# Linear attention and routed experts on one core: more buffers for the loads of q, k and v

## The chip, the cores and the metric

The kernel runs on one core of one Trainium2 chip. The metric is the device time of one execution in microseconds (us), lower is better; a time below is the median of several executions unless it is said to be the profiled one.

## The reference, cut to what matters

Eight batches with eight heads each, 576 positions, head width 64. Queries and keys are projected to 128 features, shifted by the row's largest magnitude and exponentiated with both signs; the attention is linear, so the keys and values are first summed up into one small matrix per head. The result, 4608 rows of 512, goes through a layer of eight experts of which each row takes one, or none.

```python
def phi(x):
    proj = np.einsum('bhsd,df->bhsf', x, w_phi)
    proj = proj - np.max(np.abs(proj), axis=-1, keepdims=True)
    return np.concatenate([np.exp(proj), np.exp(-proj)], axis=-1)
q_p, k_p = (phi(q), phi(k))
kv = np.einsum('bhsf,bhsd->bhfd', k_p, v)
z = np.sum(k_p, axis=2)
num = np.einsum('bhsf,bhfd->bhsd', q_p, kv)
den = np.einsum('bhsf,bhf->bhs', q_p, z)[..., None] + 1e-06
...
x = attn_out.transpose(0, 2, 1, 3).reshape(B * S, H * D)
do_compute = x @ w_skip > 0            # the other rows are returned as they are
e_idx = argmax(x @ w_gate)             # one expert for each row
y = gate_w * (relu(x @ w1[e]) @ w2[e])
out[do_compute] = x + y
```

## The kernel before, in words

**Two stages.** The attention takes the first 373 us of the profiled execution, the experts the rest. The change touches only the attention's loads.

**Units and steps.** The attention works on units: four heads of one batch, once as a k unit (k rows with their v) and once as a q unit. There are 16 units of each kind, k0 to k15 and q0 to q15. Each is cut into five items: item 0 is the tail of 64 positions of each head, items 1 to 4 are the others. The program walks in steps (line 732); in one step one item of the k stream and one of the q stream are worked on, the q stream six steps behind. One unit of each kind takes five steps, about 22 us here.

**The path of an item.** SyncE (SP) issues the load of a unit's raw rows as four transfers of 144 KB together, `raw` (`st_load`, L261 to L269). VectorE (DVE) transposes it into `xT`, or for the tail into `xTt` (L296, L298). TensorE (PE) projects it into `ps_P` (L321). DVE takes the row's largest magnitude `m` (L328) and subtracts it, which gives `u` (L331). ScalarE (ACT) exponentiates: k items straight from `u` into `ek` or `ekt` (L346, L347), q items after PE has transposed `u` into the one bank `ps_U` (L367, then L373 and L374 into `eq`). For k, PE multiplies `ek` with the values `v` into `ps_K` (L389, and L396 with the tail `vt`), and GpSimd (POOL) sums `ek` (L354). For q, PE multiplies `eq` with the unit's sums `kva` (L487, tails L466), and DVE divides: `den`, `rec`, `xm`, `lgm` (L438 to L450).

**After every batch** (two units) comes `post` (L515): DVE finds the expert of each row, PE counts ranks (L582), DVE turns them into indices (`RKH`, L607), POOL makes `OP` and `rhs` of them (L605, L617) and PE multiplies these (L628). Batches with an odd number have the tails of both batches in it and are longer. SP stores the batch's rows: half of `xm` after the first unit (L505), the rest with L566 to L568, and the output rows with L637 and L642 (1 MB and twice 128 KB).

**Buffers.** A tile has a number of buffers and takes them in turn; a load into a buffer waits until the last reader of the tile that had it before is done. `raw` has four for k and q units together, taken in the order k0, k1, q0, k2, q1, k3, q2 and so on. `v` has the two of its pool `ld`, `vt` is one of two tiles that are cleared once at the start (L94, L105) and written in two halves (L282).

**The order of the instructions** on PE is written out by hand for nearly the whole attention (L735). On DVE, POOL, SP and ACT a scheduler sets it when the program is built: it runs the program on a model of the engines and puts next what would be ready then. A transpose of a tail can so stand far ahead of the step that asks for it. On the chip each engine works through its list in that order, and an instruction whose data isn't there holds all that stand behind it.

Of the kernel before, what the change touches and what calls it, by code (L numbers as in the profile page):

```python
# [8 lines left out]
F32 = mybir.dt.float32  # L9
# [9 lines left out]
P = 128  # L19
# [5 lines left out]
def kernel(  # L25
# [13 lines left out]
    B, H, S, D = q.shape  # L39
# [34 lines left out]
    ac = pools["ac"]  # L74
# [16 lines left out]
    nc.scalar.activation(out=warm, in_=warm, func=AF.Exp)  # L91


    vts = [ac.tile([P, 2, 2, D], F32, name="vt%d" % j) for j in range(2)]  # L94
    wsrc = ac.tile([P, NF], F32, name="wsrc")

    NP2 = H // 2
# [132 lines left out]
    with actx:  # L230
        ld, hl, zp, up, ep, kvp, xp = (pools[nm] for nm in ("ld", "hl", "zp", "up", "ep", "kvp", "xp"))
# [16 lines left out]
        for b in range(B):  # L248
            for kind in ("k", "q"):
                for hq in range(NQ):  # L250
                    u = Unit()
# [8 lines left out]

        def st_load(u):  # L261
            src = kv_in[u.kind]
            u.raw = ld.tile([P, 2, 18, 32], F32, tag="raw", name="raw", bufs=4)
            for hd in range(2):
                for dh in range(2):
                    r = hd * 64 + dh * 32
                    nc.sync.dma_start(
                        out=u.raw[r:r + 32].rearrange("p r t c -> p (r t) c"),
                        in_=src[u.g, hd][:, :, dh * 32:dh * 32 + 32])  # L269

        def st_loadv(u):
            u.v = ld.tile([P, 4, 4 * D], F32, tag="v", name="v")
            u.vt = vts[u.g % 2]
            for h in range(4):
                nc.sync.dma_start(
                    out=u.v[:, h, :].rearrange("p (g c) -> p g c", c=D),
                    in_=vu[u.g, 0:4 * P, h, :].rearrange("(g p) c -> p g c", p=P))
# [423 lines left out]
        for dh in range(2):  # L701
            nc.scalar.dma_start(
                out=wsrc[dh * 64:dh * 64 + 64],
                in_=w_phi)
        st_load(streams[0][1][0])
        load_gate()

# [12 lines left out]
        def f_t():  # L720
            for items, us, off in streams:
                s = now[0] - off
                if s == CFG["ql"]:
                    st_load(us[0])
                if 0 <= s < n:
                    u, i = items[s]
                    st_t(u, i)
                    if i == 0 and s // 5 + 1 < len(us):
                        st_load(us[s // 5 + 1])

        man = None
        for t in range(n + OFF + LA):
            if CFG["man"] and t == CFG["man"][0]:
                man = ExitStack()
                man.enter_context(tc.manual_schedule(engines={mybir.EngineType.PE}))  # L735
            if CFG["man"] and t == CFG["man"][1]:
                man.close()
            now[0] = t
            for w, f in [x for x in later if x[0] <= t]:
                later.remove((w, f))  # L740
                f()
            for c in CFG["order"]:
                if c == "Z":
                    run_stage(LZ, st_z)
                elif c == "A":
                    run_stage(LA, st_aug)
                elif c == "U":
                    run_stage(LU, f_use)
                elif c == "E":
                    run_stage(LE, f_exp)  # L750
                elif c == "P":
                    st_proj()
                else:
                    f_t()
            run_stage(LU - 3, lambda u, i: st_loadv(u) if (i == 0 and u.kind == "k") else None)
            run_stage(CFG["vtl"], lambda u, i: st_loadvt(u) if (i == 0 and u.kind == "k") else None)
            if t == CFG["at"]:
                setup_aug()
            if t == 1:
                setup()  # L760
# [431 lines left out]
    with tc.manual_schedule():  # L1192
# [4 lines left out]
        for k, (w, x, c) in enumerate(steps):  # L1197
# [5 lines left out]
            while nxt < len(steps) and nxt <= k + 5 and (nxt <= k + 1 or parted[nxt] <= T[k] + 1.0):  # L1203
                w_, x_, c_ = steps[nxt]
                v = nxt not in CFG["gp"] if x_[0] == "E" else not (
                    (x_[0] == "C" and w_ == 1 or x_[0] == "S") and c_ % 2 == 1)
# [87 lines left out]
```

## Time and profile before

| what | value |
|---|---|
| median of 3 runs | 664.88 us (663.05 to 673.61) |
| the profiled execution | 655.62 us |
| its span, first to last instruction | 653.8 us |
| PE busy, of the span | 578.6 us (88%) |
| DVE busy, of the span | 515.1 us (79%) |
| loads of raw k and q | 64 transfers of 144 KB each, median 3.1 and 4.1 us from issue to landing |
| loads of v | 64 transfers of 128 KB, median 2.7 us |

A row of the timeline gives the start and the length of a piece of work in us, its engine and line, what is written from what, and in brackets how long the engine stood idle ahead of it and what ended that. "SPq" rows are transfers that SP issues; their length is the time that issuing took, not that of the transfer. A row of the waits gives the sum of such idle times, how many there were, and the longest.

### The profile page before, as it was taken

Reading aid. Unit: us, or ns where it says so; the run is one execution under the profiler, and the core shown is the slowest. Engines: PE = TensorE matmul, PEld = TensorE weight load, DVE = VectorE, ACT = ScalarE, POOL = GpSimd, SP = SyncE. Lnnn points to the kernel's source line nnn. Section 1 sums busy time; section 2 is a strip of 40 time slices with the busy share of each in tenths; the row PEclk is TensorE's granted clock in tenths of the full one; section 3 lists DMA queues with packets and bytes.
Section 4 is the critical chain, followed back from the end, with each engine's and each line's share of the span. In section 5 each row is a group of like instructions: output and inputs, shape, how many; then the busy total and the mean of one; then the engine's idle time right before and its main releaser. Section 6 shows DMA issues by size and latency. Waiting matters only on the chain. (4 is left out here: it accounts for less than half of the span.)

```text
span 653.8 us, 18749 instructions
## 1 busy us (share of the span) xinstructions
PE 578.6 (88%) x7486; PEld 473.8 (72%) x7486; DVE 515.1 (79%) x1084; ACT 329.4 (50%) x649; POOL 360.3 (55%) x389
## 2 busy tenths in 40 slices
PE   4769988979988899889899899879999898999994
PEld 2557767756776677667677788769988777998893
DVE  5668987998888969879898669995787888866761
ACT  3345554555455455445554634414457735774630
POOL 5545454654565554635666254995565958268221
PEclk9899999989999999999899989789999999999998
DMA  9977566746765756555316288858767797776300
GB/s 155 167 122 142 112 143 124 164 105 125 182 122 99 189 108 146 116 115 142 106 34 223 80 242 306 291 192 258 213 184 224 235 313 245 246 246 231 132 18 28
DMA packets 245369, 108.33 MB, mean 166 GB/s; under 512 B 192161, under 2 KB 226081, under 8 KB 245280
## 3 DMA queue, kind: packets, MB, share of 16 engines
q1 hardware_dynamic: 240768, 97.58, 57.5%
q0 software_dynamic: 3200, 9.45, 4.2%
q8 instruction: 60, 0.98, 0.6%
q10 hardware_dynamic: 1312, 0.08, 0.1%
q14 instruction: 29, 0.24, 0.1%
HBM read 83.86 MB, written 24.02 MB: 165 GB/s over the span
## 5 line engine op out<-in xcount | busy, mean ns | idle before, releaser
L354 POOL TENSOR_TENSOR z<-ek 128x512 f32<-128x512 f32 x64 | 81.4, 1272 | 122.9 <-ACT ek L347 85.2
L203 POOL TENSOR_TENSOR w<-wraw_c,w 128x256 fp32r<-128x256 f32 x124 | 112.6, 942 | 52.0 <-ACT w L198 52.0
L198 ACT ACTIVATE w<-wraw_c 128x1024 fp32r<-128x1024 f32 x96 | 97.5, 1050 | 4.2 <-DMA wraw_c<-in_moe_w_dram 3.2
L203 DVE TENSOR_TENSOR w<-wraw_c,w 128x1024 fp32r<-128x1024 f32 x65 | 86.6, 1342 | 13.1 <-ACT w L198 12.1
L331 DVE TENSOR_TENSOR u<-ps_P,m 128x1024 f32<-128x1024 f32 (+2 forms) x86 | 89.6, 1042 | 4.9 <-DVE m L328 0.5
L328 DVE TENSOR_REDUCE m<-ps_P 128x8 f32<-128x1024 f32 (+2 forms) x86 | 88.4, 1028 | 6.0 <-PE ps_P L321 5.8
L321 PE MATMUL ps_P<-wsrc,xT 64*64 64x128 f32 x2048 | 81.9, 292 | 12.0 <-DVE xT L298 7.0
L487 PEld LDWEIGHTS ps_O<-kva,eq 128*64 128x64 f32 x2048 | 74.5, 136 | 16.7 <-issue 5.5
L487 PE MATMUL ps_O<-kva,eq 128*64 128x74 f32 x2048 | 77.6, 228 | 3.9 <-DVE lgm L450 3.8
L321 PEld LDWEIGHTS ps_P<-wsrc,xT 64*64 64x64 f32 x2048 | 59.8, 140 | 28.0 <-issue 18.5
L389 PE MATMUL ps_K<-ek,v 128*64 128x256 f32 x512 | 73.9, 408 | 0.0
L851 POOL DMA_INDIRECT out_dram<-o,si x22 | 30.7, 1396 | 63.7 <-DVE si L850 57.0
L918 PE MATMUL ps_O<-w,hh 128*128 128x512 f32 x160 | 64.5, 403 | 1.3 <-DVE si L850 1.3
L346 ACT ACTIVATE ek<-u 128x512 f32<-128x512 f32 x64 | 40.4, 631 | 47.9 <-DVE u L331 35.8
L373 ACT ACTIVATE eq<-ps_U 128x512 f32<-128x512 f32 x64 | 37.8, 591 | 49.7 <-PE ps_U L367 49.2
L367 PE MATMUL ps_U<-ident,u 128*128 128x128 f32 x288 | 49.4, 289 | 13.3 <-ACT eq L374 11.0
L389 PEld LDWEIGHTS ps_K<-ek,v 128*64 128x64 f32 x512 | 32.9, 142 | 22.4 <-issue 13.1
L923 PE MATMUL ps_O<-w,hlo 128*128 128x512 f32 x120 | 47.5, 396 | 0.0
L922 PE MATMUL ps_O<-w,hh 128*128 128x512 f32 x120 | 47.4, 395 | 0.0
L367 PEld LDWEIGHTS ps_U<-ident,u 128*128 128x128 f32 x288 | 30.3, 141 | 23.5 <-ACT eq L374 12.1
L298 DVE STREAM_TRANSPOSE xT<-raw 128x512 f32<-128x512 f32 x64 | 44.5, 697 | 2.2 <-DMA raw<-in_k_dram 1.9
L905 PE MATMUL ps_P<-x,w 128*128 128x256 f32 x144 | 38.8, 299 | 4.7 <-DVE x L782 4.7
(259 smaller groups left out, 1219.5 us busy)
## 6 DMA issues: line engine op xcount, KB each, us to landing
wraw_c<-in_moe_w_dram SPq DMA_DIRECT2D x96, 512.0 KB, 4.8
raw<-in_k_dram SPq DMA_DIRECT2D x64, 144.0 KB, 3.1
raw<-in_q_dram SPq DMA_DIRECT2D x64, 144.0 KB, 4.1
v<-in_v_dram SPq DMA_DIRECT2D x64, 128.0 KB, 2.7
out_dram<-xm SPq DMA_DIRECT2D x8, 1024.0 KB, 5.2
xrows<-xm SPq DMA_DIRECT2D x8, 516.0 KB, 4.3
xrows<-xm SPq DMA_DIRECT2D x8, 512.0 KB, 4.9
vt<-in_v_dram SPq DMA_DIRECT2D x32, 32.0 KB, 2.5
```

Of the source, the lines that this page charges most:

```text
L198: nc.scalar.activation(out=hi, in_=raw, func=AF.Copy)
L203: eng.tensor_tensor(out=lo[:, r], in0=raw[:, r], in1=hi[:, r].bitcast(F32), op=ALU.subtract)
L321: nc.tensor.matmul(p[s * 64:s * 64 + 64, hd, (nj + j) * NF:(nj + j + 1) * NF], xT[r, g * P + s * 64:g * P + s * 64 + 64], wsrc[r], start=T ...
L328: nc.vector.tensor_reduce(out=m.rearrange("p (j h) -> p j h", h=2), in_=pv, axis=AX.X, op=ALU.max, apply_absolute_value=True)
L331: nc.vector.tensor_tensor(out=uu[:, 0:2 * nj, :].rearrange("p (j h) f -> p j h f", h=2), in0=pv, in1=m.rearrange("p (j h o) -> p j h o", h ...
L354: zeng.tensor_tensor(out=z, in0=e[:, 0:2, :], in1=e[:, 2:4, :], op=ALU.add)
L367: nc.tensor.transpose(t[:, tt * P:(tt + 1) * P], uu[:, tt, :], ident)
L389: nc.tensor.matmul(o[hd * 64:hd * 64 + 64, :], u.v[:, 2 * hd + pr, g * D:(g + 1) * D], u.e[i][:, 2 * j + hd, :], start=(g == 0), stop=False,)
L487: nc.tensor.matmul(ov[s * 64:s * 64 + 64, 2 * j + hd, :], e[:, half, j, hd, s * 64:s * 64 + 64], kva[:, half, 2 * pr + hd, :], start=(half ...
L918: nc.tensor.matmul(y[sub], hh[:, t], wh[:, fi, :], start=first, stop=False)
L922: nc.tensor.matmul(y[sub], hh[:, t], wl[:, fi, :], start=False, stop=False)
L923: nc.tensor.matmul(y[sub], hlo[:, t], wh[:, fi, :], start=False, stop=last)
```

## The change

`raw` has six buffers instead of four, `v` three instead of two, and there are three tiles `vt` instead of two. No operation of the steps is added or taken away; one more tile is cleared at the start.

```diff
-    vts = [ac.tile([P, 2, 2, D], F32, name="vt%d" % j) for j in range(2)]
+    vts = [ac.tile([P, 2, 2, D], F32, name="vt%d" % j) for j in range(3)]
...
-            u.raw = ld.tile([P, 2, 18, 32], F32, tag="raw", name="raw", bufs=4)
+            u.raw = ld.tile([P, 2, 18, 32], F32, tag="raw", name="raw", bufs=6)
...
-            u.v = ld.tile([P, 4, 4 * D], F32, tag="v", name="v")
-            u.vt = vts[u.g % 2]
+            u.v = ld.tile([P, 4, 4 * D], F32, tag="v", name="v", bufs=3)
+            u.vt = vts[u.g % 3]
```

The order on PE and on ACT stays as it was, apart from the names of buffers. On DVE the tails' transposes move, and on SP the loads. Numbers in names below count tiles in the order of the program, and the changed program counts two more than the one before: raw_2677 before and raw_2679 now are the same unit.

DVE in the middle of the attention, before, from the last transpose of k7 (raw_1930), which frees the buffer for k9 (raw_2677), to the tail of k9:

```order
L298 STREAM_TRANSPOSE xT_2505<-raw_1930 128x512
L331 TENSOR_TENSOR u_2209<-ps_P_2190,m_2207 128x1024
L438 TENSOR_SCALAR den_2235<-ps_O_2218 128x4
L442 RECIPROCAL rec_2236<-den_2235 128x4
L449 TENSOR_TENSOR xm_1990<-ps_O_2218,rec_2236 128x2x2x64
L450 TENSOR_TENSOR lgm_1991<-ps_O_2218,rec_2236 128x2x18
L298 STREAM_TRANSPOSE xT_2594<-raw_2002 128x512
L328 TENSOR_REDUCE m_2275<-ps_P_2258 128x8
L331 TENSOR_TENSOR u_2277<-ps_P_2258,m_2275 128x1024
L296 STREAM_TRANSPOSE xTt_3062<-raw_2677 128x128
```

The same place now. The buffer of k7 (raw_1932) goes to k10 (raw_3066), and the piece shown begins seven rows after the transpose that frees it:

```order
L328 TENSOR_REDUCE m_2277<-ps_P_2260 128x8
L331 TENSOR_TENSOR u_2279<-ps_P_2260,m_2277 128x1024
L298 STREAM_TRANSPOSE xT_2746<-raw_2301 128x512
L328 TENSOR_REDUCE m_2336<-ps_P_2323 128x6
L296 STREAM_TRANSPOSE xTt_3135<-raw_2750 128x128
L331 TENSOR_TENSOR u_2338<-ps_P_2323,m_2336 128x768
L438 TENSOR_SCALAR den_2363<-ps_O_2346 128x4
L442 RECIPROCAL rec_2364<-den_2363 128x4
L449 TENSOR_TENSOR xm_1992<-ps_O_2346,rec_2364 128x2x2x64
L450 TENSOR_TENSOR lgm_1993<-ps_O_2346,rec_2364 128x2x18
L328 TENSOR_REDUCE m_2411<-ps_P_2398 128x6
L296 STREAM_TRANSPOSE xTt_3419<-raw_3066 128x128
```

From the transpose that frees a buffer to the tail that reads what was loaded into it there were 9 rows here, and are now 18. From k7 and q6 on these distances were 7 to 23 rows; now they are 18 to 33 for k units and 49 to 64 for q units (23 for the last one). Both tails now stand between an `m` and its `u`.

DVE at the start, now: k5 is raw_1190.

```order
L298 STREAM_TRANSPOSE xT_953<-raw_557 128x512
L328 TENSOR_REDUCE m_656<-ps_P_639 128x8
L296 STREAM_TRANSPOSE xTt_1575<-raw_1190 128x128
L331 TENSOR_TENSOR u_658<-ps_P_639,m_656 128x1024
L438 TENSOR_SCALAR den_685<-ps_O_668 128x4
```

Before, the tail of k5 stood 14 rows further down, behind the second `u` and all the divisions that follow here; the rows around it are otherwise the same.

SP at the start, before, from the load of q2 (raw_555) to that of q4 (raw_1259); k4 is raw_813 and k5 raw_1188:

```order
L267 DMA raw_555<-in_q_dram 32x36x32 x4
L282 DMA vt0_102<-in_v_dram 64x2x64
L275 DMA v_560<-in_v_dram 128x4x64 x4
L282 DMA vt0_102<-in_v_dram 64x2x64
L267 DMA raw_813<-in_k_dram 32x36x32 x4
L267 DMA raw_882<-in_q_dram 32x36x32 x4
L282 DMA vt1_103<-in_v_dram 64x2x64
L275 DMA v_887<-in_v_dram 128x4x64 x4
L282 DMA vt1_103<-in_v_dram 64x2x64
L267 DMA raw_1188<-in_k_dram 32x36x32 x4
L505 DMA xrows_93<-xm_543 512x1x256
L267 DMA raw_1259<-in_q_dram 32x36x32 x4
```

The same place now, two loads further, to the first store:

```order
L267 DMA raw_557<-in_q_dram 32x36x32 x4
L275 DMA v_562<-in_v_dram 128x4x64 x4
L282 DMA vt2_104<-in_v_dram 64x2x64 x2
L267 DMA raw_815<-in_k_dram 32x36x32 x4
L267 DMA raw_884<-in_q_dram 32x36x32 x4
L275 DMA v_889<-in_v_dram 128x4x64 x4
L282 DMA vt0_102<-in_v_dram 64x2x64 x2
L267 DMA raw_1190<-in_k_dram 32x36x32 x4
L267 DMA raw_1261<-in_q_dram 32x36x32 x4
...
L267 DMA raw_1577<-in_k_dram 32x36x32 x4
L505 DMA xrows_93<-xm_545 512x1x256
```

The loads of k, q and v come in the same turn as before, with the tails of v no longer split around v here. What moved are the stores: the first one stood behind k5 and now stands behind k6 (raw_1577), and so on to the end, so that at each store SP has loaded one unit more. In the experts' stage no row has moved on any engine. The experts' tiles lie in the memory that the attention's pools leave, and since those pools are larger now, they lie over other tiles of the attention than before.

## The prediction

> **What bounds the kernel now.** Only the attention's loads change, so I asked first which engine that stage waits for. Its regular part runs from 50 to 330 us. The table by stretches (length, busy time of PE, its weight loads, DVE, ACT and POOL, granted clock, DMA share, GB/s) and the waits of PE in the same stretch (sum, count, longest):
>
> ```profile
> 50.00:330.00 280.00, 252.34 (x4704) 194.65 (x4700) 240.01 (x565) 147.03 (x348) 149.30 (x136) 0.98 0.60 131
> ```
>
> ```profile
> PE ps_O L628 <- POOL rhs L617: 10.2, 6, 2.5
> PE ps_O L582 <- DVE lgm L450: 6.9, 6, 2.8
> PE ps_U L367 <- ACT eq L374: 6.5, 4, 2.3
> PE ps_O L487 <- DVE lgm L450: 3.8, 3, 1.5
> ```
>
> PE is busy for 252.3 of 280 us, and these four rows hold 27.4 of the 27.7 us in which it isn't. None names a load. The loads stand one engine further back, in the waits of DVE and then of SP's queue, again from 50 to 330 us:
>
> ```profile
> DVE xTt L296 <- DMA raw<-in_q_dram: 20.9, 9, 3.6
> DVE xTt L296 <- DMA raw<-in_k_dram: 5.5, 6, 1.5
> ```
>
> ```profile
> SPq L275 <- PE ps_K L389: 53.1, 12, 6.3
> SPq L267 <- DVE xT L298: 36.4, 12, 5.7
> ```
>
> DVE stands 26.4 us in front of tails that haven't landed. SP issues these loads late because it waits for a buffer: for `v` until PE has used the one two units back, for `raw` until DVE has transposed the one four back. So PE sets the pace where nothing stalls, DVE follows closely (240 of 280 us), and a late load costs what DVE can't make up before PE needs it. One such chain, in order of time, from four timelines:
>
> ```profile
> 190.85 5.37 SPq L267 DMA_DIRECT2D raw<-in_q_dram  x4
> ```
>
> ```profile
> 198.60 0.31 DVE L296 STREAM_TRANSPOSE xTt<-raw 128x128 f32<-128x128 f32 x1 [3.35 <-DMA raw<-in_q_dram]
> ```
>
> ```profile
> 199.85 0.42 ACT L346 ACTIVATE ekt<-u 128x256 f32<-128x256 f32 x1 [4.89 <-DVE den L438]
> ```
>
> ```profile
> 201.59 0.66 PE L367 MATMUL ps_U<-ident,u 128*128 128x128 f32 x4 [2.12 <-ACT eq L374]
> ```
>
> The tail of q10 holds DVE for 3.35 us; the next `u` comes after it, ACT's `ekt` needs that `u`, `eq` stands behind `ekt` in ACT's list, and PE waits 2.12 us for `eq` to leave the bank `ps_U`. That tail isn't asked for until a unit later: the scheduler had put it there because its model had it landed.
>
> **The change part by part.** *What it removes.* A load now waits for the transposes six back, and the tails that read it stand 18 to 33 rows (k) or 49 to 64 rows (q) behind that point. Whether this is enough is read at the tightest place, k10, which now gets the buffer that k7's last transpose frees:
>
> ```profile
> 143.80 0.70 DVE L298 STREAM_TRANSPOSE xT<-raw 128x512 f32<-128x512 f32 x1
> ```
>
> ```profile
> 144.53 2.67 SPq L267 DMA_DIRECT2D raw<-in_k_dram  x4
> ```
>
> ```profile
> 151.27 0.31 DVE L296 STREAM_TRANSPOSE xTt<-raw 128x128 f32<-128x128 f32 x1 [1.40 <-DMA raw<-in_k_dram]
> ...
> 154.94 0.31 DVE L296 STREAM_TRANSPOSE xTt<-raw 128x128 f32<-128x128 f32 x1 [0.86 <-DMA raw<-in_q_dram]
> ...
> 155.99 0.95 DVE L328 TENSOR_REDUCE m<-ps_P 128x6 f32<-128x768 f32 x1
> ```
>
> Freed at 144.50, issued from 144.53 on and landed at 151.27: 6.8 us. The tail will stand behind the `m` that ends at 156.94, or 154.7 without the two stalls ahead of it: 10.2 us after the release. That leaves 3.4 us. For q units even 49 rows (some 25 us by half a microsecond a row) stand against the 5.4 us of issuing and 2 us of landing above. I expect no stall from 60 us on; at worst k units keep theirs, 5.5 us.
>
> What this is worth on PE goes by its four rows. *L367, 6.5 us:* three of the four waits, and all but 0.3 us of the sum, stand behind q stalls like the one shown; I take 6.2. *L487, 3.8 us:* each is behind a stall, as here:
>
> ```profile
> 243.64 0.31 DVE L296 STREAM_TRANSPOSE xTt<-raw 128x128 f32<-128x128 f32 x1 [3.00 <-DMA raw<-in_q_dram]
> ```
>
> ```profile
> 251.58 1.25 PE L487 MATMUL ps_O<-kva,eq 128*64 128x74 f32 x32 [1.42 <-DVE lgm L450]
> ```
>
> I take all 3.8. *L582 and L628, 17.1 us,* are the ranks after a batch, in an even batch (DVE's row, then PE's) and in an odd one:
>
> ```profile
> 176.50 0.31 DVE L296 STREAM_TRANSPOSE xTt<-raw 128x128 f32<-128x128 f32 x1 [2.16 <-DMA raw<-in_q_dram]
> ```
>
> ```profile
> 177.69 0.19 PE L582 MATMUL ps_O<-Stot,ones_b 128*128 128x32 bf16 x1 [0.90 <-DVE lgm L450]
> ...
> 183.61 0.35 PE L628 MATMUL ps_O<-rhs,OP 128*128 128x32 bf16 x8 [1.64 <-POOL rhs L617]
> ```
>
> ```profile
> 221.08 0.19 PE L582 MATMUL ps_O<-Stot,ones_b 128*128 128x40 bf16 x1 [0.73 <-DVE lgm L450]
> ...
> 227.91 0.43 PE L628 MATMUL ps_O<-rhs,OP 128*128 128x32 bf16 x10 [2.52 <-POOL rhs L617]
> ```
>
> The even wait at L582 comes with the stall of 2.16 us, and goes with it. The odd wait has no stall right ahead of it, but DVE has no gap between 198.6 and 228 us, so it would come there up to 3.35 us earlier. The waits at L628 end a chain of their own, from the ranks through DVE and POOL, which gets shorter only where DVE was late. Bounds: nothing to 17.1. I take 4 of 6.9 and 2 of 10.2, nearer the lower end, since the work of `post` stays.
>
> *What it adds.* One more clearing of a `vt` on POOL in the first microseconds, whose cover is that its load comes third, after 35 us; I take nothing. And a stall at the start. SP's rows, then DVE's, then PE's:
>
> ```profile
> 36.82 2.98 SPq L267 DMA_DIRECT2D raw<-in_k_dram  x4
> 39.90 4.37 SPq L267 DMA_DIRECT2D raw<-in_q_dram  x4
> 44.37 0.85 SPq L282 DMA_DIRECT2D vt<-in_v_dram  x1
> 50.65 2.30 SPq L275 DMA_DIRECT2D v<-in_v_dram  x4
> ```
>
> ```profile
> 43.33 0.31 DVE L296 STREAM_TRANSPOSE xTt<-raw 128x128 f32<-128x128 f32 x1 [3.42 <-DMA raw<-in_k_dram]
> ...
> 50.26 1.19 DVE L328 TENSOR_REDUCE m<-ps_P 128x8 f32<-128x1024 f32 x1
> ```
>
> Until 45 us SP issues without a pause, so no buffer holds it and the stalls of the first units (3.42 us at k4) stay. Then it paused for `v` until 50.65; now it goes on: `v` (2.3 us) and two `vt` (0.6 to 0.85 each) end at 48.0, k5 at 51.0, landed 3.5 us after that, as k4 was, at 54.5. But k5's tail now stands behind the `m` that ends at 51.45: up to 3.0 us of stall, ahead of a `u`. After that PE has no idle time for a while, so DVE has some lead and part is made up:
>
> ```profile
> 52.00:70.00 18.00, 18.00 (x332) 13.72 (x332) 14.33 (x30) 10.38 (x25) 8.93 (x7) 1.00 0.64 127
> ```
>
> Bounds 0 and 3.0, I take 2.
>
> *Sum:* 6.2 + 3.8 + 4 + 2 − 2 = 14.0 us. The span becomes 653.8 − 14.0 = 639.8, that execution 655.6 − 14.0 = 641.6, and the median of the runs shown, which lies 9.3 us above it, 664.9 − 14.0 = 650.9: **651 us**. The experts' stage only starts earlier. Its own range: from 9 (the ranks give nothing, the start costs 1) to 20 us.
>
> One rule leads elsewhere. The Trainium skill, "Perfetto Trace Analysis", Identifying the Most-Contended Engine, says that TensorE's matmul busy share isn't a fair measure, and that VectorE's occupancy is. By it DVE's 86% would set the pace and each stalled microsecond would be paid. That is the rival next below; the row from 52 to 70 us speaks against it, with PE busy for all 18 us and DVE for 14.3.
>
> **The rivals.** *DVE sets the pace.* Then all 26.4 us less the 2 at the start come off: 640 us. For it: DVE's stretch without a gap in the odd batch. Against: only 27.4 us of PE's time are idle, and 10.2 of that end with POOL. With it I count the case that the clock's dips go too, in these stretches:
>
> ```profile
> 228.00:234.00 6.00, 6.00 (x116) 4.50 (x119) 3.93 (x9) 2.65 (x7) 4.89 (x4) 0.73 0.06 11
> 290.00:296.00 6.00, 5.40 (x114) 4.30 (x114) 5.65 (x12) 3.81 (x9) 1.27 (x1) 1.00 0.25 57
> ```
>
> After the odd batch's 0.73 and 2.52 us of idling PE ran at 0.73 for 6 us, which is 1.6 us lost; after the longest wait at L367, 2.3 us, it did not. Three odd batches make 4.8 us, if their waits shrink enough: 651 − 4.8 = 646. The Trainium skill, "TensorE: Matmul & The Clock Gate", What's actually happening, has the clock halved after an idle window of about 3.4 us; by that the dip hangs on the two waits together, and would go.
>
> *The stalls move and the ranks' chain stays.* L582 and L628 give nothing, and k units keep half their stalls: 10.0 − 2 − 3 = 5 us, 660 us. For it: the scheduler again puts each tail where its model, too early before, has it landed. Against: 3.4 us left at the tightest place. That the change does nothing at all would need the old distances, and they have doubled.
>
> *Slower.* Each tail now stands ahead of a `u` that ACT and PE wait for; a stall there is paid in full. If the loads of k5 to k15 stall as q loads do now (20.9 over 9, or 2.3 us), that is 11 × 2.3 = 25.5 us, against the 16 us that go: 664.9 + 9.5 + 2 = 676 us. It decides from loads that land more than 10.2 us after their release, 3.4 later than shown. Nothing queued ahead of a k load grew, so this is unlikely.
>
> **How the numbers follow.** The forecast 0.55; the clock's dips 0.12 and DVE as the pace 0.05, together 0.17; the smaller gain 0.23; slower 0.05. Two per cent is 13.3 us, about what a measurement of this kernel can tell from no change: faster than 651.6. Just over half of the forecast's own range and all of the greater gain lie beyond it: 0.55 × 0.5 + 0.17 = 0.44, of which I take 0.42 as the runs spread over 10 us. Slower by 2% needs 678, half of the last case: 0.03. The rest is 0.55. The range takes in both neighbours: 638 to 663 us.
>
> **What would show it.** In the changed profile DVE's waits for raw q and k from 60 us on should fall from 26 us to under 4; PE's waits at L367 and L487 to under 2; those at L582 and L628 to 11; SP's wait for `v` should nearly go, that for `xT` should stay, since SP keeps DVE's beat. A stall of 2 to 3 us should stand ahead of k5's tail near 51 us. I am wrong if the DVE stalls go and PE's idle time doesn't, or if k tails still wait in the middle of the attention.

## The result and the profile after

| | before | after |
|---|---|---|
| median | 663.96 us (661.23 to 673.61, 4 runs) | 641.24 us (640.84 to 641.75, 4 runs) |
| the profiled execution, its span | 655.62 us, 653.8 us | 640.84 us, 638.8 us |
| first instruction of the experts (L778) | 373.3 us | 358.8 us |
| the rest of the span | 280.5 us | 280.0 us |

The ratio is 0.967, with an interval from 0.964 to 0.971: the changed kernel is faster. The profiled execution lost 15.0 us of span, 14.5 of them in the attention.

The table by stretches of the changed kernel, from 50 to 330 us (length, busy time of PE, its weight loads, DVE, ACT and POOL, granted clock, DMA share, GB/s), the waits of PE there (sum, count, longest), and those of DVE:

```profile
50.00:330.00 280.00, 265.97 (x4966) 206.25 (x4964) 254.28 (x607) 154.33 (x363) 158.97 (x144) 0.98 0.60 131
```

```profile
PE ps_O L628 <- POOL rhs L617: 7.7, 6, 2.4
PE ps_O L487 <- DVE lgm L450: 3.0, 1, 3.0
PE ps_O L582 <- DVE lgm L450: 2.2, 3, 0.7
```

```profile
DVE m L328 <- PE ps_P L321: 9.0, 17, 1.7
DVE xT L298 <- PE ps_P L321: 5.4, 12, 0.9
DVE xTt L296 <- DMA raw<-in_k_dram: 2.8, 1, 2.8
```

PE is busy for 266.0 of 280 us instead of 252.3. The row for L367 has shrunk to 0.2 us, and the 3.0 us at L487 are now one wait. DVE's 26.4 us in front of tails are gone but for one, and what DVE waits for now is PE: 14.4 us in two rows. The one wait that is left stands at the start, as the timeline of the changed kernel shows (issue of k5's load, DVE's tail, PE):

```profile
48.35 2.75 SPq L267 DMA_DIRECT2D raw<-in_k_dram  x4
...
54.63 0.31 DVE L296 STREAM_TRANSPOSE xTt<-raw 128x128 f32<-128x128 f32 x1 [2.76 <-DMA raw<-in_k_dram]
...
57.03 1.26 PE L487 MATMUL ps_O<-kva,eq 128*64 128x74 f32 x16 [3.02 <-DVE lgm L450]
```

SP's waits from 50 to 330 us, after:

```profile
SPq L275 <- PE ps_K L389: 37.2, 10, 6.2
SPq L267 <- DVE xT L298: 22.8, 9, 5.1
```

SP still waits 37.2 us for a buffer of `v`, although there are three.

The gain isn't spread evenly. Two stretches, before and then after:

```profile
0.00:60.00 60.00, 42.52 (x628) 29.40 (x632) 41.29 (x75) 25.85 (x59) 31.92 (x54) 0.94 0.82 143
60.00:300.00 240.00, 215.39 (x4073) 166.88 (x4070) 203.31 (x485) 125.45 (x294) 125.77 (x114) 0.99 0.62 133
```

```profile
0.00:60.00 60.00, 39.20 (x570) 27.16 (x570) 38.21 (x71) 22.90 (x51) 29.62 (x53) 0.91 0.92 159
60.00:300.00 240.00, 232.14 (x4369) 180.60 (x4368) 220.48 (x528) 135.17 (x320) 135.97 (x123) 0.99 0.64 141
```

In the first 60 us PE does less than before (39.2 us against 42.5), in the next 240 us 16.8 us more. So the change wins in the middle and loses at the start.

### The profile page after: what moved, and what is told of

Read it like the earlier page. It is cut to its first block, busy times and chain, and to the rows that moved or that the text cites. A ratio compares the mean times of both kernels' runs of the same rounds, so it can differ in the third digit from the quotient of the medians.

```text
span 638.8 us, 18742 instructions
## 1 busy us (share of the span) xinstructions
PE 577.4 (90%) x7486; PEld 473.5 (74%) x7486; DVE 514.4 (81%) x1084; ACT 329.1 (52%) x649; POOL 360.5 (56%) x390
## 5 line engine op out<-in xcount | busy, mean ns | idle before, releaser
L487 PEld LDWEIGHTS ps_O<-kva,eq 128*64 128x64 f32 x2048 | 76.6, 140 | 16.7 <-issue 6.2
L487 PE MATMUL ps_O<-kva,eq 128*64 128x74 f32 x2048 | 79.8, 232 | 3.1 <-DVE lgm L450 3.0
L389 PE MATMUL ps_K<-ek,v 128*64 128x256 f32 x512 | 72.2, 400 | 0.0
L367 PE MATMUL ps_U<-ident,u 128*128 128x128 f32 x288 | 50.0, 291 | 7.6 <-ACT eq L374 4.3
L367 PEld LDWEIGHTS ps_U<-ident,u 128*128 128x128 f32 x288 | 30.7, 143 | 17.7 <-ACT eq L374 4.6
```

The lines of the kernel that those rows point to most:

```text
L367: nc.tensor.transpose(t[:, tt * P:(tt + 1) * P], uu[:, tt, :], ident)
L389: nc.tensor.matmul(o[hd * 64:hd * 64 + 64, :], u.v[:, 2 * hd + pr, g * D:(g + 1) * D], u.e[i][:, 2 * j + hd, :], start=(g == 0), stop=False,)
L487: nc.tensor.matmul(ov[s * 64:s * 64 + 64, 2 * j + hd, :], e[:, half, j, hd, s * 64:s * 64 + 64], kva[:, half, 2 * pr + hd, :], start=(half ...
```

## The experiments

What was to be settled: whether `raw` or `v` brings the gain, and whether it is the number of buffers that counts or the place where the scheduler had put the tails' transposes. My theory is the second: a tail that stands early on DVE holds everything behind it until it lands, and more buffers only let the load land sooner. The main rival is that the loads themselves have to run further ahead.

Spans are those of the profiled executions. All ratios are against runs of before on the same chip.

| run | what it is | median us | ratio, interval | span us | first L778 us |
|---|---|---|---|---|---|
| e1 | six raw | 638.35 | 0.970 (0.965 to 0.976) | 634.9 | 354.9 |
| e2 | three v | 665.28 | 1.008 (1.005 to 1.012) | 663.8 | 383.7 |
| e3 | four raw, two `xTt` | 626.96 | 0.953 (0.947 to 0.959) | 624.0 | 344.7 |
| e4 | the change, two `xTt` | 641.42 | 0.975 (0.970 to 0.980) | 637.2 | 356.6 |
| e5 | five raw | 644.59 | 0.971 (0.964 to 0.978) | 638.1 | 360.7 |
| e6 | six raw, two `xTt` | 635.14 | 0.955 (0.949 to 0.961) | 635.2 | 352.4 |
| e7 | e4, store on ACT's queue | 638.88 | 0.959 (0.952 to 0.966) | 637.8 | 355.9 |
| e8 | five raw, two `xTt` | 632.62 | 0.952 (0.945 to 0.958) | 631.1 | 348.8 |
| e9 | e4, store later | 642.24 | 0.970 (0.963 to 0.977) | 641.5 | 361.2 |
| e10 | e3, store later | 631.91 | 0.959 (0.952 to 0.966) | 628.1 | 347.6 |
| e11 | the change, store later | 642.85 | 0.975 (0.969 to 0.981) | 639.9 | 359.5 |
| e12 | e9, three xm | 627.66 | 0.948 (0.939 to 0.956) | 627.8 | 345.2 |

### e1 and e2: one part alone

```diff
-            u.raw = ld.tile([P, 2, 18, 32], F32, tag="raw", name="raw", bufs=4)
+            u.raw = ld.tile([P, 2, 18, 32], F32, tag="raw", name="raw", bufs=6)
```

> Six buffers for raw alone; v and its tails keep two. Theory A (DVE stands at tails that were put too far ahead, and the distance from the release of a raw buffer to its tail sets the stall): these distances are those of the full change from k7 on (18 to 33 rows for k, 49 to 64 for q), so the whole gain comes with raw: 0.97 of the time before, within 1% of the full change; DVE waits for raw after 60 us under 4 us. Rival B (what held SP was v: 53 us of SP's queue waited for PE to free a v, and the raw loads stand behind v in that queue): then raw alone gives less than half, over 0.985, and DVE's waits for raw stay above 10 us.

And the two other parts of the change, `v` with three buffers and three tiles `vt`, alone:

```diff
-            u.v = ld.tile([P, 4, 4 * D], F32, tag="v", name="v")
-            u.vt = vts[u.g % 2]
+            u.v = ld.tile([P, 4, 4 * D], F32, tag="v", name="v", bufs=3)
+            u.vt = vts[u.g % 3]
```

> Three buffers for v and three tiles for its tails; raw keeps four. Theory A: the distances on DVE from k7 on are the old ones (7 to 23 rows), so DVE still stands some 20 us in front of the tails from 60 us on and the time is within 1% of before. Rival B: SP's wait for v (53 us) goes, the raw loads behind it are issued earlier, and half or more of the gain comes: 0.985 or less.

PE's waits from 60 to 300 us with six `raw` alone, the only two rows above 1 us:

```profile
PE ps_O L628 <- POOL rhs L617: 7.7, 6, 2.4
PE ps_O L582 <- DVE lgm L450: 2.2, 3, 0.7
```

From 50 to 330 us too they are 7.7 and 2.2 us, as in the full change, and DVE has no wait for `raw` from 60 us on. With three `v` alone DVE's waits for tails from 60 to 300 us are as before:

```profile
DVE xTt L296 <- DMA raw<-in_q_dram: 21.5, 11, 2.8
DVE xTt L296 <- DMA raw<-in_k_dram: 5.9, 6, 2.0
```

What follows: the whole gain is that of `raw`, as theory A has it in both texts. Three buffers of `v` give nothing, and alone they cost 0.8%. A part of that is the start, where they put the next load of `v` ahead of that of k4; DVE's timeline of that kernel:

```profile
46.49 0.31 DVE L296 STREAM_TRANSPOSE xTt<-raw 128x128 f32<-128x128 f32 x1 [4.76 <-DMA raw<-in_k_dram]
```

The longest wait for a k load in before was 3.42 us. In the first 60 us PE does 4.0 us less than in before (38.5 against 42.5). The rest of the 10.4 us by which this attention ends later lies behind that. From 60 to 300 us PE's waits are about the same as in before and the granted clock is 0.96 instead of 0.99; no run ties that to the buffers.

### e3: the order instead of the buffers

```diff
-            xT = hl.tile([P, n], F32, tag="xT" + sfx, name="xT" + sfx)
+            xT = hl.tile([P, n], F32, tag="xT" + sfx, name="xT" + sfx, bufs=2 if sfx else None)
```

All buffers are as in before; only the transposed tails `xTt` have two instead of the five of their pool. The scheduler then can't place a tail's transpose before the last but one `xTt` has been read. From k7 on every tail now stands 55 to 71 rows of DVE behind the release of its raw buffer, against 7 to 23 in before. In the built programs only the order on DVE differs from before; on PE, ACT, POOL and SP no row has moved.

> The kernel before with its four and two buffers, but only two tiles xTt for the tails' transposes instead of five: the scheduler can then not put a tail's transpose far ahead, and it stands 55 to 71 rows behind the release of its buffer and at most 12 rows ahead of the unit's next transpose. Theory A: the stalls on raw go without any buffer more, and the time is that of the full change or 2 to 6 us lower, as the stalls at k4 and k5 at the start go too. Rival C (the loads themselves have to come a unit earlier, that is what more buffers give): the load of a unit is no earlier than before, so DVE still waits over 10 us for raw, only at another place, and the time is within 1% of before.

The stretches 0 to 60 and 60 to 300 us of this kernel:

```profile
0.00:60.00 60.00, 48.61 (x798) 34.96 (x800) 46.88 (x87) 30.84 (x70) 35.81 (x57) 0.97 0.91 159
60.00:300.00 240.00, 230.00 (x4331) 178.42 (x4329) 221.88 (x532) 136.03 (x322) 138.24 (x127) 0.99 0.65 143
```

With four raw buffers the middle is as busy as with six (230.0 us against 230.1 in e1), and the start is better by 9.4 us of PE: the stalls of the first units, which six buffers leave where they were, are gone as well but for 2.8 us at two q tails. This kernel beats the changed one: span 624.0 against 638.8. That is 14.8 us lower, far more than the 2 to 6 us that I expected. So the number of buffers was never what was short. A tail's transpose stood too early in an order that can't be left, and six buffers were one way to have its load landed by then.

### e4, e6 and e8: both together, and why that is worse

The same edit on top of the full change (e4), of six raw buffers alone (e6) and of five (e8).

> The full change and two tiles xTt. Theory A: in the middle of the attention nothing is left to gain (no DVE wait for raw there already); what goes is the stall of 2.8 us at the tail of k5 and the 3.0 us of PE behind it, perhaps the 3.2 and 4.0 us at k4: 3 to 7 us under the full change, 634 to 638 us. Rival C: the same as the full change within 2 us, since the start is bound by the rate at which SP issues and the transfers land.

> Before with six raw buffers and two buffers for the transposed tail rows, v as in before. It asks why six buffers with the short tail lost 13 us against four buffers with it. Theory (the store L505 of the first half of xm stands behind one more unit's loads on SyncE's queue; VectorE's next write of that tile waits for it): here too the store stands after the load of one more unit, so VectorE waits 10 us or more at L449 near 60 us, and the span is 634 to 640. Rival (the third buffer of v lets SyncE run the loads of v ahead of the store): without it the store goes out near 53 us as with four buffers, the wait is under 3 us, and the span is 624 to 628.

> Before with five raw buffers and two buffers for the transposed tail rows. On SyncE's queue the store L505 stands where it stands with four buffers and the short tail, and the loads run one buffer ahead. Theory (once the transposes are not placed early, a further buffer has nothing left to give, and a store that keeps its place costs nothing): span 622 to 627, VectorE's waits for raw between 60 and 300 us from 2.8 us to 0 or nearly, the wait at L449 under 4 us. Rival (any buffer more pushes the loads ahead of the store in time): VectorE waits 8 us or more at L449 and the span is 632 or more.

e4 did not go on from e3, it lost 13 us to it. Its span of 637.2 lies where both of its forecasts put it, but neither had the wait that brought it there: the stalls at the start are gone, as theory A said, and one new wait of DVE costs as much. In order of the kernels e3, e8, e6 and e4, from the timeline of each: the store of the first half of `xm` (L505) on SP, and DVE's next write of that tile, with its wait in brackets:

```profile
52.59 0.56 SPq L505 DMA_DIRECT2D xrows<-xm  x1
57.01 0.42 DVE L449 TENSOR_TENSOR xm<-ps_O,rec 128x256 f32<-128x256 f32 x1 [1.78 <-DMA xrows<-xm]
```

```profile
56.22 0.66 SPq L505 DMA_DIRECT2D xrows<-xm  x1
61.13 0.42 DVE L449 TENSOR_TENSOR xm<-ps_O,rec 128x256 f32<-128x256 f32 x1 [5.63 <-DMA xrows<-xm]
```

```profile
59.95 0.76 SPq L505 DMA_DIRECT2D xrows<-xm  x1
64.74 0.42 DVE L449 TENSOR_TENSOR xm<-ps_O,rec 128x256 f32<-128x256 f32 x1 [9.30 <-DMA xrows<-xm]
```

```profile
64.30 0.71 SPq L505 DMA_DIRECT2D xrows<-xm  x1
69.05 0.42 DVE L449 TENSOR_TENSOR xm<-ps_O,rec 128x256 f32<-128x256 f32 x1 [13.49 <-DMA xrows<-xm]
```

In the built programs 64, 68, 72 and 78 transfers of raw, `v` and `vt` stand ahead of that store on SP's queue: each raw buffer more puts a load of four ahead of it, the third `v` six more. The store leaves 3.6, 3.7 and 4.4 us later from one kernel to the next, DVE waits 3.9, 3.7 and 4.2 us longer, and the end of the attention goes from 344.7 to 348.8, 352.4 and 356.6 us. The cost goes with the number of transfers ahead, step by step; from e3 to e8 no row has moved in the built programs but on SP. The steps are those of the traces and of the medians (627.0, 632.6, 635.1 and 641.4 us). The ratios show only the last (0.953, 0.952, 0.955, 0.975), as before took a median of 664.7 us on the chip of e8 and e6 and 658.9 on that of e3 and e4. My expectation for five buffers was wrong here: I had taken the store's place in the queue for unchanged, and overlooked the one load more ahead of it; the 5.6 us lie between the bounds of the theory and of the rival. For six, the rival that `v` was needed for it is out, as e6 has no third `v` and waits 9.3 us, just under the 10 that I expected.

### e7: the store on another queue

```diff
-                        nc.sync.dma_start(out=rowm[b][:, :, c], in_=xm[:, :, c])
+                        nc.scalar.dma_start(out=rowm[b][:, :, c], in_=xm[:, :, c])
```

> The full change with two buffers for the transposed tail rows, and the store of the first half of xm (L505) issued by ScalarE's queue instead of SyncE's. Theory (only the store's place behind the loads costs the 13.5 us wait of VectorE, and 9 us of TensorE's): the wait at L449 near 60 us falls under 3 us, and the span from 637 to between 624 and 629. Rival (the store is late because the loads ahead fill the 16 transfer engines, not because of its place in the queue): it goes out early but lands late, VectorE still waits 8 us or more, and the span stays at 633 to 638. A third: ScalarE waits ahead of the store for VectorE's result and its exponentials come late, which would show as new waits of GpSimd and TensorE for ScalarE of 3 us and more.

ACT's timeline:

```profile
49.44 0.63 ACT L347 ACTIVATE ek<-u 128x512 f32<-128x512 f32 x1
59.59 0.59 ACTq L505 DMA_DIRECT2D xrows<-xm  x1
60.23 0.41 ACT L425 ACTIVATE kva<-ps_O 128x292 f32<-128x292 f32 x1 [10.16 <-DMA v<-in_v_dram]
```

The store was next on ACT at 50 us, and DVE had written its last data by 49.3. It left at 59.59 all the same. The built program gives it two waits, one for DVE and one for a DMA semaphore:

```
66 L505 DMA xrows_93<-xm_545 512x1x256 [waits DMAHW0_49,DVE_49]
```

(66 is its row on ACT.) That for DVE was fulfilled at 49.3; what is left is the DMA semaphore. The program gives its transfers eight such semaphores in turn, whichever engine issues them, and in the attention each transfer waits for the one eight places ahead of it. For this store that is one of the four transfers of a load of `v` that SP issued from 56.12 to 58.32 us; the profile too names a load of `v`. So the store's place in the order of all transfers hadn't changed with the queue. DVE's wait shrank to 0.7 us, but ACT's `kva` stood behind the store and PE waited 6.5 us for it. The span stayed at 637.8. So the theory that only the place on SP's queue counts fell. The effect of the third outcome came about, ACT late and PE waiting for it, but for another reason than named there: ACT waited for a transfer and not for DVE, and `kva` was late and not the exponentials.

### e9 to e12: no write behind the store

```diff
-                    later.append((now[0] + 2, store_half))
+                    later.append((now[0] + 6, store_half))
```

Four steps later the store stands behind DVE's writes of the second half, and no write of the same batch waits for it. On e4 (e9), on e3 (e10) and on the change alone (e11):

> The full change with two buffers for the transposed tail rows, and the store of the first half of xm (L505) issued four steps later, behind VectorE's writes of the second half of that tile, so that no write waits for it. What moved the store to another queue showed: there it went out at 59.6 us all the same, behind its DMA semaphore, and ScalarE's own work stood behind it. Theory (the write of the second half that waits for the store of the first is all that six buffers with the short tail lose): the wait of 13.5 us at L449 near 60 us is gone, TensorE's wait at L487 with it, 60 to 80 us has TensorE busy 19 us and more against 10.9, and the span is 623 to 628 against 637.2. Rival (the loads that run further ahead hold up something else, v or its tail, as soon as the store is out of the way): another wait of VectorE or TensorE of 4 us and more stands between 50 and 80 us and the span is 630 to 637.

> Before with two buffers for the transposed tail rows (four raw buffers, two of v) and the store of the first half of xm four steps later. With four buffers that store cost VectorE 1.8 us and TensorE nothing. Theory: within 2 us of the same kernel without the move, span 622 to 626, and equal within 2 us to six buffers with the same two edits, so that the number of buffers gives nothing once transposes and store are out of each other's way. Rival (six buffers still bring something at four buffers' remaining 2.8 us of waits for raw): four buffers are 3 us or more behind six.

> The full change with only the store of the first half of xm moved four steps later; the transposed tail rows keep their five buffers. In the changed kernel VectorE waited 0.6 us for that store, because the transposes that stand early had made it late already. Theory: no change, span 637 to 640, the wait of 3 us at L487 near 57 us stays with the wait for raw that causes it. Rival (the store was a part of the start's loss): TensorE's waits below 60 us shrink by 2 us and more and the span is under 636.

In e9 DVE's wait at L449 was gone, and in the first 80 us PE was busy for 68.2 us, as in e3 (68.6), against 57.2 in e4. But the next stores of the batch stand behind the same loads, and two batches later the same buffer of `xm` is written again. The timeline of e9 (SP, ACT, PE):

```profile
86.04 1.59 SPq L566 DMA_DIRECT2D xrows<-xm  x1
91.40 0.21 ACT L561 ACTIVATE xm<-sid 128x4 f32<-128x4 f32 x1 [12.21 <-DMA xrows<-xm]
92.64 0.69 PE L367 MATMUL ps_U<-ident,u 128*128 128x128 f32 x2 [7.96 <-ACT eq L374]
```

So the theory's signs came and its span did not: it was 641.5, and a wait of the kind that the rival meant was there, but behind its 80 us, at ACT's write of `xm` (L561) and not for `v`, and the span lies above the rival's 637 too. In e10, with four raw buffers, ACT's wait at this place is 5.4 us and the span 628.1, 4.1 more than without the edit instead of within 2 (2.9 of them in the attention). Nor is it equal to six buffers with the same edits: e9 lies 13.4 us above it. In e11 nothing changed, as expected: 639.9 against 638.8. There DVE had waited 0.6 us for the store; the stalls of the first units come ahead of it and stay (39.1 us of PE in the first 60 us). The last run takes ACT's wait away too, by a third buffer:

```diff
-                    xp.tile([P, 4, XW], F32, tag="xm", name="xm"),
+                    xp.tile([P, 4, XW], F32, tag="xm", name="xm", bufs=3),
```

> The full change with two buffers for the transposed tail rows, the store of the first half of xm four steps later, and a third buffer of xm. In the kernel without the third buffer ScalarE waited 12.2 us near 91 us: its write of the xm tile of the third batch waits for the store of the first batch's second half (L566), which stood on SyncE's queue behind one more unit's loads, and TensorE lost 8 us there. Theory (the stores of xm behind loads that run further ahead are all that six buffers with the short tail lose, and every such store had a write waiting behind it): with a third buffer no write waits for a store of the batch just done, ScalarE's wait at L561 is under 3 us, 80 to 100 us has TensorE busy 19 us and more against 11.8, and the span is 623 to 629. Rival (the transfers themselves are too late, so that another reader waits): a wait of 4 us or more stands on TensorE between 80 and 130 us at another line, and the span is 632 or more.

The stretches 0 to 80 and 80 to 100 us of e12 (in e9 the second of them had 11.80 us of PE at 0.74):

```profile
0.00:80.00 80.00, 68.32 (x1173) 49.88 (x1176) 66.23 (x140) 42.07 (x97) 46.18 (x66) 0.98 0.90 161
80.00:100.00 20.00, 19.77 (x392) 15.58 (x388) 18.55 (x44) 11.36 (x27) 13.07 (x13) 1.00 0.89 188
```

ACT has no wait at L561 any more, and the attention ends at 345.2 us. In the built programs no row stands elsewhere than in e9. Of the 16.0 us between the two, 10.2 are waits of PE at L367 that are gone (10.4 to 0.2 us from 30 to 340 us); the clock of e9 was low too, 0.57 from 86 to 98 us. So the writes that wait for late stores are what e4 had lost to e3, and with them gone the full change with two `xTt` comes to where four raw buffers with two `xTt` had been: 627.66 and 626.96 us, 345.2 and 344.7 us. Six raw buffers, three `v` and three `xm` buy nothing over the one edit of e3.

### e5: five raw buffers

> Before with five raw buffers instead of four, nothing else. From the tenth unit on, the two-row transpose stands 11 to 27 rows of VectorE behind the last read of its buffer, against 7 to 23 in before and 18 to 64 with six. VectorE runs 528 rows in 220.5 busy us there, 0.42 us a row, so the least gap goes from 2.9 to 4.6 us, and the waits of before, up to 3.6 us, end 1.7 us and more earlier. Theory (a wait is as long as the load is slower than this gap): the waits for raw between 60 and 300 us fall from 26.4 us to between 3 and 8, TensorE's waits at L367 and L487 behind 60 us to under 2, and the span is 637 to 643, most of the way from 654 to six buffers' 635. Rival (the loads need to be two units ahead, whatever the order): about half of the gain, 14 us of waits for raw left and a span of 645 or more.

DVE's waits for tails from 60 to 300 us:

```profile
DVE xTt L296 <- DMA raw<-in_k_dram: 4.0, 5, 1.6
DVE xTt L296 <- issue: 1.5, 1, 1.5
```

5.5 us are left of 26.4 (for 1.5 of them the profile names nothing that DVE waited for), and PE has no wait at L367 or L487 above 0.2 us. The span of 638.1 us lies in the range of the theory. The distance by which a load has to lead is short here: five buffers, with 11 to 27 rows, give most of what six give with 18 to 64. The rival's 14 us didn't come.

## Why the prediction was right, point by point

- **PE's four rows.** L367 was to give 6.2 us and gave 6.3. L487 was to give 3.8, and in the middle it did; its 3.0 us after are the new stall at the start. L582 was to give 4 and gave 4.7 (6.9 to 2.2), L628 2 and gave 2.5 (10.2 to 7.7). All four together: 17.3 us against 16.
- **The stall at the start.** It came where it was said to: k5's load from 48.35 to 51.10, its tail landed at 54.6, and 2.76 us of DVE. I had charged 2 us, on the ground that DVE has some lead. PE waited 3.02 us and ran at a granted clock of 0.57 from 56 to 60 us; over the first 60 us it did 3.3 us less. This term was mis-sized, by 1.3 us. 17.3 − 3.3 = 14.0 against 14.5 measured at the end of the attention.
- **SP's wait for `v`.** "Should nearly go" was wrong: 53.1 to 37.2 us, and to 42.8 in e1, which has no third `v`. The wait for `xT`, which was to stay, fell from 36.4 to 22.8 us. SP is ahead of the engines that it feeds, and it has to wait for some buffer; a third one moves the wait by a unit, it doesn't end it. None of PE's time hung on it, so it did no harm to the sum.
- **DVE as the pace.** Out: of 26.4 us of DVE's waits 15 reached the span, and DVE now waits 14.4 us for PE. By the rule of the Trainium skill, "Perfetto Trace Analysis", Identifying the Most-Contended Engine, DVE's occupancy would have been the measure; here PE's idle time was, with 97% of 60 to 300 us busy after.
- **The clock's dips.** They did not go with the change: three after odd batches before, three after. But they are not bound to the waits either, as the next section but one shows.
- **From the span to the median.** The sum gave 641.6 us for an execution like the profiled one, and that of the changed kernel took 640.84. The forecast of 651 added the 9.3 us by which the median of before lay above its profiled execution, as if they were the program's. This is the step that failed. The four executions of the changed kernel lie within 0.9 us. Of 33 later executions of before the median is 660.7 us, from 656.0 to 667.8: the profiled one was shorter than all of them. Why before spreads so much and the changed kernel doesn't is not shown; at mean clocks of 0.962 to 0.969 before took 656.7 to 664.7 us.
- **The range.** That it holds 641.2 us is luck in part. The forecast's own range, a gain of 9 to 20 us, ends at 645; the stated range goes down to 638 for the sake of two rivals, the clock's dips at 646 and DVE as the pace at 640. The measured time lies next to the second of these, whose mechanism the traces speak against.
- **The cause.** The tails that stand early on DVE were named as the cause, and e3, in which only the order on DVE differs, shows it. What the prediction did not ask is whether the order could be changed instead of the buffers.

## What to carry to other kernels

Where a scheduler places a read early on an engine that works in order, the read's data must have landed on the chip, and not in the scheduler's model; fewer buffers for the result of that read (two `xTt` instead of five, 32 us off the median of before on the same chip) can do more than more buffers for its source. More buffers for loads put more loads ahead of a store in the order of the transfers, at 0.7 to 0.9 us each here, and another queue did not help; before adding some, look for a write that waits for such a store. A wait of the queue that feeds the engines was no sign here that buffers are short: look whether anyone waits for what it issues.

## What the runs showed of the hardware that was not expected

**Dips of the clock come in equal pieces, and not behind every equal wait.** After the long wait of an odd batch PE's clock drops, or it doesn't. The starts at L628 in the first two odd batches, from PE's timelines of the changed kernel and then of e1:

```profile
137.12 0.40 PE L628 MATMUL ps_O<-rhs,OP 128*128 128x32 bf16 x10 [2.37 <-POOL rhs L617]
...
219.59 0.40 PE L628 MATMUL ps_O<-rhs,OP 128*128 128x32 bf16 x10 [2.36 <-POOL rhs L617]
```

```profile
136.17 0.40 PE L628 MATMUL ps_O<-rhs,OP 128*128 128x32 bf16 x10 [2.38 <-POOL rhs L617]
...
217.16 0.40 PE L628 MATMUL ps_O<-rhs,OP 128*128 128x32 bf16 x10 [2.37 <-POOL rhs L617]
```

The stretches of 6 us right behind them, in the same order:

```profile
137.50:143.50 6.00, 6.00 (x111) 4.44 (x109) 4.56 (x11) 2.35 (x7) 4.61 (x4) 0.72 0.30 49
220.00:226.00 6.00, 6.00 (x110) 4.41 (x109) 4.45 (x11) 2.46 (x7) 4.56 (x4) 0.72 0.20 33
```

```profile
136.50:142.50 6.00, 6.00 (x123) 4.74 (x120) 5.12 (x12) 3.90 (x10) 4.67 (x4) 1.00 0.33 54
217.50:223.50 6.00, 6.00 (x123) 4.72 (x120) 5.13 (x12) 4.01 (x10) 4.67 (x5) 1.00 0.36 58
```

The waits are the same to 0.02 us, and one kernel runs at 0.72 behind both, the other at full clock. From one L628 to the other it is 82.47 us with a dip and 80.99 without: 1.48 us a dip. e3 has both in one execution: its first two odd batches have waits of 2.37 us each, and the next L628 comes 80.99 us behind the first of them, at full clock, and 82.48 behind the second, with a dip. The pieces are equal: around each of the six dips of the changed kernel up to 306 us the granted clock is 0.57 over 4 us, 1.7 us short of full clock in sum. Behind the long waits of e4 and e9 it is 0.57 over 12 us (from 64 to 76 and from 86 to 98 us), three such pieces. Two dips more, 3.0 us, are most of the 3.9 us by which the full change ends its attention behind e1, so these traces leave some 1 us for the third `v` beside six raw buffers. The Trainium skill, "TensorE: Matmul & The Clock Gate", What's actually happening, says that the window in which idling is judged runs freely and isn't started by the kernel; that the same wait is hit at one place and not at another agrees with it. That chance decides is not shown, since each kernel has one trace.

**Executions of one kernel differ by their mean clock.** In e10 two at 0.979 took 629.5 and 629.8 us, one at 0.969 took 636.0; 1% of 630 us is 6.3. Of the 33 executions of before, the twelve at 0.969 and more have a median of 657.8 us, the eleven at 0.961 and less 664.5. The clock explains part of the spread (three executions at 0.967 to 0.973 took 661 us and more); what sets it in an execution was not found. The changed kernel doesn't follow it: 641.75 us at 0.962, 641.34 and 640.84 at 0.969.

**What stays open.** The stage of the experts took from 277.4 to 282.8 us in these kernels, though none of the edits touches it; it holds 3.3 of the 3.8 us between the spans of e12 and e3.
